# Mixture of experts on one core: the last two token groups with a Strassen second product, scaled left operands and kept weight parts

## The chip, the core and the metric

One Trainium2 chip, one of its cores. TensorE (PE in the profile) multiplies, with its own weight loads (PEld) beside it; VectorE (DVE), ScalarE (ACT) and GpSimd (POOL) work on tiles, and SyncE (SP) only issues transfers here. The metric is the device time of one execution in microseconds, the median of the runs.

## What is computed

Attention over 4 batches and 8 heads (queries pooled in pairs) gives 2304 tokens of 512 numbers, which pass through 8 experts. A gate P of 2304 x 8 is normalised by eight Sinkhorn rounds. Cut to what matters, with D = 512 and F = 1024:

```python
for e in range(8):
    h = np.maximum(x @ w1[e], 0.0)        # [2304, 1024]
    ye = h @ w2[e]                        # [2304, 512]
    out += P[:, e:e+1] * ye
```

All is float32. The kernel gets there on a faster matmul type (fp32r) by cutting each operand into a high part and a low remainder; a product is then three matmuls: high by high, high by low, low by high.

## The kernel before

`attention()` is a plan, a list of operations with costs that is put in order before the program is written. `moe()` is written in plain order, and a scheduler places its instructions. This case is about `moe()`.

The tokens go in G = 3 groups of TG = 768 (two halves of TH = 384). For each group the kernel walks over 32 steps, a step being one expert and one quarter of its hidden width (256 of 1024). The activations stay in one tile `x` [128, 4, 2304], with the model dimension on the partitions.

One step does this:

- **First product.** `product` makes x @ w1 for 256 hidden columns and 768 tokens by seven Strassen-Winograd block products of six matmuls each, 128x128 by 128x384 (L855 to L857, tile `psh`): 42 matmuls. The seven left operands are two parts of `w1s`, one more of it, and four sums (`w1t`, made by Pool in L133 to L136, for steps 2 to 8 of the first group by DVE). Each is cut into `w1h` (ACT, L147) and `w1l` (DVE, L152), in every group anew. The seven right operands are sums of x, cut into `xch` and `xcl` once per group (L100, L103; Pool makes the sums in L94).
- **Between.** ACT copies one block result (L870), DVE adds others (L875), and `hidden` cuts the rectified result into `hh` (ACT, L864) and `hl` (DVE, L865).
- **Second product.** Two steps make a window. In the window's wake `second` multiplies its hidden columns by w2, for each of the group's six tiles of 128 tokens 12 matmuls 128x128 by 128x512 (L885, tile `pso`): 72 in a window, 36 in a step. `w2s` is cut by ACT (L162) and DVE (L163). DVE takes each `pso` off, times its column of P, and adds it to `x` (L917; ACT in a group's first window, L911), which by then is free of the group's activations.
- **Loads and stores.** SP issues the loads of `w1s` (L119) and `w2s` (L125), 512 KB each, one of each per step, into one buffer each, and at a group's end the stores of the six token tiles (L919; the last tile in two halves, L904 and L905).

The reused buffers set the order: `w1s` can be loaded again once its cuts and sums are made, `w1h` and `w1l` have two buffers, `psh` and `pso` four each. The first product of a step needs only cuts made during the step before.

## Time and profile before

| | us |
|---|---|
| median of 3 runs | 1869.77 (1869.28 to 1870.08) |
| span of the profiled execution, first to last instruction | 1867.4 |
| PE busy | 1861.2 (100%) |
| DVE busy | 1438.6 (77%) |
| ACT busy | 825.5 (44%) |
| POOL busy | 509.2 (27%) |
| chain of work that ended last: PE | 98%, of it L885 42% |

The profiled execution's span is 2.4 us below the median. The attention part fills about the first 380 us, the three groups of 496 us each the rest. A profile's "busy" is a share over the whole span; what bounds a stage is seen from which wait ends last in it. A matmul's listed duration overlaps with its neighbours, so the cost of one is read from start to start.

### The profile page before, as it was taken

The numbers are of one execution on the slowest core, as the hardware profiler recorded it, in microseconds if no ns is written. First come the engines' busy times: TensorE is split into PE (matmuls) and PEld (weight loads), VectorE is DVE, ScalarE is ACT, GpSimd is POOL, SyncE is SP. The second block draws the span as 40 slices with busy tenths as digits, with TensorE's granted clock in tenths as the row PEclk, the third lists the DMA queues.
The fourth block names the chain that finished last, engine by engine and source line by source line (L and its number), as shares of the span: only waits on it lengthen the run. The fifth ranks groups of instructions, "written<-read, shape, count | busy, mean of one in ns | idle before, by whom it ended". The sixth has DMA issues, their size and how long they took to land.

```text
span 1867.4 us, 30970 instructions
## 1 busy us (share of the span) xinstructions
PE 1861.2 (100%) x11901; PEld 1673.9 (90%) x11901; DVE 1438.6 (77%) x2953; ACT 825.5 (44%) x1442; POOL 509.2 (27%) x504
## 2 busy tenths in 40 slices
PE   9999999999999999999999999999999999999999
PEld 8888888889999999999999999999899999999998
DVE  8999999799776767677777777777866777777774
ACT  7888887744333333333433333333433333333331
POOL 5555555410222222231222222223122222222210
PEclk9999999999999999999999999999999999999999
DMA  6777776322221212122212121212131212221211
GB/s 212 187 210 195 198 195 170 82 79 91 79 75 61 78 59 79 57 80 80 91 57 79 57 79 57 79 57 79 46 120 63 77 61 75 64 72 67 70 57 34
DMA packets 59524, 173.26 MB, mean 93 GB/s; under 512 B 11632, under 2 KB 21232, under 8 KB 59376
## 3 DMA queue, kind: packets, MB, share of 16 engines
q1 hardware_dynamic: 59088, 170.89, 30.7%
q8 instruction: 93, 1.52, 0.3%
q14 instruction: 55, 0.45, 0.1%
q10 hardware_dynamic: 288, 0.39, 0.1%
HBM read 134.81 MB, written 4.79 MB: 75 GB/s over the span
## 4 chain that ended last, share of the span: by engine, by line
PE 98%; DVE 1%; DMA 0%; ACT 0%; POOL 0%; issue 0%; POOLq 0%; ACTq 0%; SPq 0%
PE pso L885 42%; PE psh L857 12%; PE psh L855 12%; PE psh L856 12%; PE ps L530 7%; PE ps L607 4%; PE ps L639 3%; PE ps L653 3%; PE ps L658 1%; DVE w1l L152 0%; DMA w1s<-in_moe_w_dram 0%; DVE hl L865 0%; DMA qr<-in_q_dram 0%; PE ps L63 0%; ACT w1h L147 0%
## 5 line engine op out<-in xcount | busy, mean ns | idle before, releaser
L857 PE MATMUL psh<-xch,w1l 128*128 128x384 f32 x1344 | 450.2, 335 | 1.2 <-DVE w1l L152 1.2
L885 PE MATMUL pso<-w2h,hl 128*128 128x512 f32 x1156 | 450.7, 390 | 0.0
L885 PE MATMUL pso<-w2l,hh 128*128 128x512 f32 x1156 | 450.5, 390 | 0.0
L855 PE MATMUL psh<-xch,w1h 128*128 128x384 f32 x1344 | 450.1, 335 | 0.0
L856 PE MATMUL psh<-xcl,w1h 128*128 128x384 f32 x1344 | 449.6, 335 | 0.0
L885 PE MATMUL pso<-w2h,hh 128*128 128x512 f32 x1156 | 448.8, 388 | 0.0
L864 ACT ACTIVATE hh<-c 128x384 fp32r<-128x384 f32 x384 | 199.9, 522 | 377.5 <-DVE c L875 377.5
L133 POOL TENSOR_TENSOR w1t<-w1s 128x256 f32<-128x256 f32 x88 | 65.4, 743 | 1053.9 <-DMA w1s<-in_moe_w_dram 750.4
L917 DVE SCALAR_TENSOR_TENSOR x<-pso,PR,x 128x512 f32<-128x512 f32 x263 | 196.7, 748 | 158.2 <-PE pso L885 153.1
L885 PEld LDWEIGHTS pso<-w2h,hl 128*128 128x128 f32 x1156 | 217.0, 188 | 44.9
L855 PEld LDWEIGHTS psh<-xch,w1h 128*128 128x128 f32 x1344 | 252.3, 188 | 4.4 <-DVE c L875 0.4
L885 PEld LDWEIGHTS pso<-w2l,hh 128*128 128x128 f32 x1156 | 217.0, 188 | 43.1
L856 PEld LDWEIGHTS psh<-xcl,w1h 128*128 128x128 f32 x1344 | 252.3, 188 | 3.5
L885 PEld LDWEIGHTS pso<-w2h,hh 128*128 128x128 f32 x1156 | 217.1, 188 | 42.7
L857 PEld LDWEIGHTS psh<-xch,w1l 128*128 128x128 f32 x1344 | 252.2, 188 | 2.4 <-DVE w1l L152 2.4
L538 DVE TENSOR_SCALAR_CACHE_REDUCE E<-ps 128x384 f32<-128x384 f32 x432 | 214.9, 552 | 9.6 <-PE ps L530 8.6
L865 DVE SCALAR_TENSOR_TENSOR hl<-c,hh 128x384 fp32r<-128x384 f32 x384 | 211.3, 551 | 4.9 <-ACT hh L864 4.1
L870 ACT ACTIVATE p<-psh 128x384 f32<-128x384 f32 x96 | 47.2, 491 | 336.2 <-PE psh L857 335.0
L551 ACT ACTIVATE E<-E,st 128x1152 f32<-128x1152 f32 x144 | 179.9, 1262 | 16.0 <-DVE st L544 15.9
L163 DVE TENSOR_TENSOR w2l<-w2s,w2h 128x1024 fp32r<-128x1024 f32 x95 | 126.8, 1335 | 73.8 <-ACT w2h L162 73.8
L875 DVE TENSOR_TENSOR c<-psh,u 128x384 f32<-128x384 f32 x288 | 151.2, 554 | 42.1 <-PE psh L857 40.5
L162 ACT ACTIVATE w2h<-w2s 128x1024 fp32r<-128x1024 f32 x95 | 100.1, 1053 | 181.3 <-PE pso L885 181.3
(108 smaller groups left out, 2214.3 us busy)
## 6 DMA issues: line engine op xcount, KB each, us to landing
w1s<-in_moe_w_dram SPq DMA_DIRECT2D x96, 512.0 KB
w2s<-in_moe_w_dram SPq DMA_DIRECT2D x96, 512.0 KB
F<-T SPq DMA_DIRECT2D x168, 184.0 KB
qr<-in_q_dram SPq DMA_DIRECT2D x15, 640.0 KB
vt<-in_v_dram SPq DMA_DIRECT2D x16, 576.0 KB
kr<-in_k_dram SPq DMA_DIRECT2D x15, 576.0 KB
out_dram<-x SPq DMA_DIRECT2D x17, 256.0 KB
RB<-rd SPq DMA_DIRECT2D x32, 128.0 KB
```

The costliest lines, as they stand in the source:

```text
L163: self.tc.keep_in_program_order(self.nc.vector.tensor_tensor(out=lo, in0=self.raw2[k], in1=hi.bitcast(F32), op=ALU.subtract))
L530: nc.tensor.matmul(ps[h][:, :PK], D["qT", p][rows, x, t * P:(t + 1) * P], D["kT", p][rows, y, j * PK:(j + 1) * PK], start=(i == 0), stop=( ...
L538: nc.vector.tensor_scalar(out=D["E", m, h][:, j * PK:(j + 1) * PK], in0=D["sc", m, j][h][:, :PK], scalar1=0.0625, scalar2=None, op0=ALU.mu ...
L551: nc.scalar.activation(out=x, in_=x, func=ACTF.Exp, bias=D["st", m][:, h, 3:4], accum_out=sums[p % RS][:, col + h * QT:col + h * QT + 1])
L855: nc.tensor.matmul(ps, hi[:, a, c, :], blocks.xch[:, b, c, :], start=(c == 0), stop=False)
L856: nc.tensor.matmul(ps, hi[:, a, c, :], blocks.xcl[:, b, c, :], start=False, stop=False)
L857: nc.tensor.matmul(ps, lo[:, a, c, :], blocks.xch[:, b, c, :], start=False, stop=(c == 1))
L864: nc.scalar.activation(out=hh[:, fh, ts], in_=src, func=ACTF.Relu)
L865: nc.vector.scalar_tensor_tensor(out=hl[:, fh, ts], in0=src, scalar=0.0, in1=hh[:, fh, ts].bitcast(F32), op0=ALU.max, op1=ALU.subtract)
L875: nc.vector.tensor_tensor(out=y, in0=ps, in1=t, op=ALU.add)
L885: nc.tensor.matmul(ps, u[:, fh, ms], w[:, fh, ds], start=(n == 0), stop=(n == 11))
L917: nc.vector.scalar_tensor_tensor(out=a, in0=ps, scalar=PR[:, m, e:e + 1], in1=a, op0=ALU.mult, op1=ALU.add)
```

## The change

The first group stays as it was but for two things: w2 is laid out with its two halves of 256 columns apart, and after each step's cut both parts of w1 are written to a DRAM tile `w1c` (917.5 KB each, two transfers on SP ahead of the next load of `w1s`). P of groups 2 and 3 is turned once and written to DRAM (`spread`).

The last two groups leave `moe()` for a new function `late()`, a second plan:

- The high and low parts of w1 come back from DRAM in one load of 1.835 MB per step, into two buffers; nothing of w1 is summed or cut again.
- P of the expert is loaded as a row over all partitions (`pb`), and the rectified first product is multiplied by it (DVE, two operations of 384 and one of 2x384 columns per step). The sums between block products are carried by ACT copies from one PSUM bank to another; two more are added by DVE.
- The second product of a window is made by seven block products of twelve matmuls, 128x128 by 128x384 (L1193 in the new code): 84. Pool sums four blocks of w2 (512 wide) and four of h (768 wide); for each block product ACT cuts w_hi (512) and h_hi (768), DVE cuts w_lo (512) and h_lo (768), and DVE adds the result (768) to `x` (ACT in a group's first window).
- At a group's end seven sums of 768 columns (`join`, DVE or Pool) give the outputs, still with the model dimension on the partitions, and `finish` turns them by 24 matmuls against the identity, copies them out (12 copies of 256, ACT or DVE) and stores 12 pieces of 128 KB.

The diff's core:

```diff
@@ Weights.cut1, first group
             self.hi1(k)
             self.lo1(k)
+            t = self.kept[k] = self.cuts.tile([P, 2, 7, 2, P], F32, name=f"w1c{k}")
+            for i, y in enumerate(self.a[k]):
+                self.nc.sync.dma_start(out=t[:, i], in_=y.bitcast(F32))
...
+LATE_CAPS = dict(pb=2, w1=2, w2=2, w2t=1, hb=2, ht=1, hc=3, wc=3, e=2, mt=2, os=3)
...
+            def load_w1(k=k):
+                y = D0["w1", k] = tile("w1", [2, 7, 2, P], F32R)
+                nc.sync.dma_start(out=y.bitcast(F32), in_=wt.kept[k % (E * FQ)])
...
+                nc.vector.scalar_tensor_tensor(out=hb(b), in0=ps(n), scalar=0.0, in1=pb(0), op0=ALU.max, op1=ALU.mult)
...
+                nc.gpsimd.tensor_tensor(out=hblock(i), in0=D0[HB][:, a], in1=D0[HB][:, b], op=sub)
...
+                (nc.gpsimd if end else nc.vector).tensor_tensor(out=y[:, 1], in0=wsrc(), in1=y[:, 0].bitcast(F32), op=sub)
...
+                nc.vector.tensor_tensor(out=y[:, 1], in0=hblock(b), in1=y[:, 0].bitcast(F32), op=sub)
...
+                    for s in range(2):
+                        for y, z in ((0, 0), (0, 1), (1, 0)):
+                            nc.tensor.matmul(o, w[:, y, s, ds], v[:, z, s], start=(i == 0), stop=(i == 5))
```

How the instructions stand, at three places. First DVE in the steady part of a group. Before, about one step: sums (L875), the low part of h (`hl`, L865), the low parts of w1 and w2 (L152, L163), and `pso` taken off (L917).

```order
L875 TENSOR_TENSOR c_11466<-psh,c_11466 128x384
L865 SCALAR_TENSOR_TENSOR hl<-c_11475,hh 128x384
L152 TENSOR_TENSOR w1l<-w1s,w1h 128x512
L865 SCALAR_TENSOR_TENSOR hl<-c_11466,hh 128x384
L152 TENSOR_TENSOR w1l<-w1s,w1h 128x256
L152 TENSOR_TENSOR w1l<-w1t,w1h 128x1024
L917 SCALAR_TENSOR_TENSOR x<-pso,PR,x 128x4x128 x2
L163 TENSOR_TENSOR w2l<-w2s,w2h 128x1024
L917 SCALAR_TENSOR_TENSOR x<-pso,PR,x 128x4x128
L875 TENSOR_TENSOR c_11570<-psh,p_11561 128x384
```

In `late()`, under half of a window of 31 instructions: h scaled by P (L1089 and L1113, tile `hb`), w_lo and h_lo (L1170, L1180; tiles `wc`, `hc`, beside the sum tiles `w2t` and `ht`), a block product taken off (L1208, tile `mt`).

```order
L1170 TENSOR_TENSOR wc<-w2t,wc 128x512
L1113 SCALAR_TENSOR_TENSOR hb<-hb,pb 128x2x384
L1089 SCALAR_TENSOR_TENSOR hb<-bD,pb 128x384
L1208 TENSOR_TENSOR x<-mt,x 128x768
L1180 TENSOR_TENSOR hc<-hb,hc 128x768
L1170 TENSOR_TENSOR wc<-w2t,wc 128x512
L1180 TENSOR_TENSOR hc<-ht,hc 128x768
L1208 TENSOR_TENSOR x<-mt,x 128x768
L1170 TENSOR_TENSOR wc<-w2t,wc 128x512
L1180 TENSOR_TENSOR hc<-hb,hc 128x768
L1089 SCALAR_TENSOR_TENSOR hb<-bA,pb 128x384
```

The cuts of w1 are gone from DVE; wider cuts of h and of w2 stand there in turn with the results that are taken off.

Second, Pool beside it. Before, one step:

```order
L133 TENSOR_TENSOR w1t<-w1s 128x256 [waits DMAHW1_49,DVE_49]
L135 TENSOR_TENSOR w1t<-w1s 128x256
L134 TENSOR_TENSOR w1t<-w1t,w1s 128x256 [waits Pool_49]
L136 TENSOR_TENSOR w1t<-w1s,w1t 128x256 [waits Pool_49]
L133 TENSOR_TENSOR w1t<-w1s 128x256 [waits DMAHW3_49,DVE_49]
```

In `late()`, a window's eight:

```order
L1135 TENSOR_TENSOR w2t<-w_13610 128x512 [waits DMAHW4_49,DMAHW3_49,DVE_49]
L1135 TENSOR_TENSOR w2t<-w2t,w_13610 128x512 [waits Pool_49]
L1135 TENSOR_TENSOR w2t<-w_13610 128x512
L1135 TENSOR_TENSOR w2t<-w_13610,w2t 128x512 [waits Pool_49]
L1151 TENSOR_TENSOR hb<-hb 128x768 [waits DVE_49]
L1151 TENSOR_TENSOR ht<-hb 128x768 [waits DVE_49]
L1151 TENSOR_TENSOR hb<-hb 128x768 [waits Pool_49]
L1151 TENSOR_TENSOR hb<-hb 128x768 [waits DVE_49,Pool_49]
```

Eight short sums for two steps have become four of double and four of triple width, the last four fed by DVE.

Third, SP where the first group ends. Before, the stores of the finished tiles (L919) lie among the loads:

```order
L125 DMA w2s<-in_moe_w_dram 128x1024
L119 DMA w1s<-in_moe_w_dram 128x1024
L125 DMA w2s<-in_moe_w_dram 128x1024
L919 DMA out_dram<-x 512x1x128 x3
L119 DMA w1s<-in_moe_w_dram 128x1024
L919 DMA out_dram<-x 512x1x128
L125 DMA w2s<-in_moe_w_dram 128x1024
L919 DMA out_dram<-x 512x1x128 x2
```

Now, from the first group's last steps on (kept parts L163, loads L122 and L128, stores L913, then `pb` L1037, the kept parts back L1051, w2 L1043):

```order
L122 DMA w1s<-in_moe_w_dram 128x1024
L128 DMA w2s<-in_moe_w_dram 128x1024
L163 DMA w1c_10346<-w1h 128x1792
L163 DMA w1c_10346<-w1l 128x1792
L128 DMA w2s<-in_moe_w_dram 128x1024
L913 DMA out_dram<-x 512x1x128 x5
L1037 DMA pb<-spread 128x768
L913 DMA out_dram<-x 512x1x128
L1051 DMA w_10650<-w1c_5992 128x3584
L1043 DMA w_10658<-in_moe_w_dram 128x1024 x2
L1051 DMA w_10673<-w1c_6084 128x3584
```

In the first group two writes now stand ahead of each load of `w1s`; at its end all six stores, each behind DVE, stand ahead of the first load of `late()`.

## Rows read from the trace of the kernel before

**Rows 1.** the page: busy us (share), and the chain that ended last

```profile
PE 1861.2 (100%) x11901; PEld 1673.9 (90%) x11901; DVE 1438.6 (77%) x2953; ACT 825.5 (44%) x1442; POOL 509.2 (27%) x504
...
PE 98%; DVE 1%; DMA 0%; ACT 0%; POOL 0%; issue 0%; POOLq 0%; ACTq 0%; SPq 0%
```

**Rows 2.** chain of waits, 1000 to 1035: start us, us, engine, tile, line

```profile
1002.19 8.20 PE pso L885 x36
1017.69 8.20 PE pso L885 x36
```

**Rows 3.** engines in windows, steady: us, busy us (count), PEclk, DMA share, GB/s

```profile
1000.00:1015.50 15.50, 15.50 (x80) 14.06 (x79) 11.27 (x18) 5.33 (x9) 3.72 (x4) 1.00 0.21 69
```

**Rows 4.** DVE by line and form: count | busy us, mean ns | idle

```profile
L152 DVE TENSOR_TENSOR w1l<-w1s,w1h 128x512 fp32r<-128x512 f32 x95 | 66.3, 698 | 0.1
L103 DVE TENSOR_TENSOR xcl<-x,xch 128x768 fp32r<-128x768 f32 x9 | 8.4, 950 | 0.0
L875 DVE TENSOR_TENSOR c<-psh,p 128x384 f32<-128x384 f32 x96 | 53.5, 557 | 80.6 <-PE psh L857 80.0 <-ACT w1h L147 0.5
L913 DVE TENSOR_TENSOR x<-pso,x 128x512 f32<-128x512 f32 x6 | 3.9, 687 | 0.0
L865 DVE SCALAR_TENSOR_TENSOR hl<-c,hh 128x384 fp32r<-128x384 f32 x384 | 211.3, 551 | 4.9 <-ACT hh L864 4.1
L163 DVE TENSOR_TENSOR w2l<-w2s,w2h 128x1024 fp32r<-128x1024 f32 x95 | 126.8, 1335 | 73.8 <-ACT w2h L162 73.8
```

**Rows 5.** POOL in order of time, 1287 to 1294: start us, us, engine, line

```profile
1288.95 0.74 POOL L134 TENSOR_TENSOR w1t<-w1t,w1s 128x256 f32<-128x256 f32 x1
1289.77 1.61 POOL L136 TENSOR_TENSOR w1t<-w1s,w1t 128x256 f32<-128x256 f32 x1
1291.33 1.85 POOL L94 TENSOR_TENSOR xt<-x,xt 128x768 f32<-128x768 f32 x1
```

**Rows 6.** DVE in order of time, 1289 to 1302

```profile
1289.28 1.49 DVE L163 TENSOR_TENSOR w2l<-w2s,w2h 128x1024 fp32r<-128x1024 f32 x1 [1.71 <-ACT w2h L162]
1290.69 0.74 DVE L917 SCALAR_TENSOR_TENSOR x<-pso,PR,x 128x512 f32<-128x512 f32 x1
1291.72 0.56 DVE L875 TENSOR_TENSOR c<-psh,p 128x384 f32<-128x384 f32 x1 [0.29 <-PE psh L857]
1300.33 0.75 DVE L917 SCALAR_TENSOR_TENSOR x<-pso,PR,x 128x512 f32<-128x512 f32 x1
1300.99 1.22 DVE L163 TENSOR_TENSOR w2l<-w2s,w2h 128x1024 fp32r<-128x1024 f32 x1
```

**Rows 7.** POOL, then DVE, 362 to 372

```profile
366.24 1.83 POOL L94 TENSOR_TENSOR xt<-x 128x768 f32<-128x768 f32 x1
368.02 2.13 POOL L707 TENSOR_TENSOR x<-x,RB 128x576 f32<-128x576 f32 x1
...
367.09 3.89 DVE L103 TENSOR_TENSOR xcl<-xt,xch 128x768 fp32r<-128x768 f32 x2
```

**Rows 8.** ACT by line and form: count | busy us, mean ns | idle

```profile
L100 ACT ACTIVATE xch<-xt 128x768 fp32r<-128x768 f32 x8 | 6.7, 840 | 0.6 <-POOL xt L94 0.3
```

**Rows 9.** SP, then POOL, in order of time, 1000 to 1017

```profile
1004.80 0.33 SPq L119 DMA_DIRECT2D w1s<-in_moe_w_dram  x1
...
1008.40 0.73 POOL L133 TENSOR_TENSOR w1t<-w1s 128x256 f32<-128x256 f32 x1 [12.62 <-DMA w1s<-in_moe_w_dram]
```

**Rows 10.** engines in windows: with stores and loads; after the end

```profile
878.00:880.00 2.00, 2.00 (x12) 1.84 (x11) 0.75 (x1) 0.00 (x0) 1.92 (x3) 1.00 0.91 301
1866.00:1867.40 1.40, 0.00 (x0) 0.00 (x0) 0.00 (x0) 0.00 (x0) 0.00 (x0) 0.53 0.06 18
```

**Rows 11.** PE at the start, in order of time; chain, 240 to 256

```profile
1.56 3.79 PE L401 MATMUL ps<-ident 128*128 128x128 f32 x16 [1.56 <-POOL ident masks.py:199]
...
243.89 2.81 PE ps L607 x24
```

**Rows 12.** the last piece of the chain of waits

```profile
1864.19 0.48 DVE x L904
```

More of the change, by code (lines that the diff above doesn't have):

```diff
@@ L43, in attention_moe @@
         tc.tile_pool(name="const", bufs=1) as const,
[L44 removed]
+        tc.tile_pool(name="cuts", bufs=1, space=bass.MemoryType.DRAM) as cuts,
     ):
+        stage = tc.alloc_tile_pool(name="stage", bufs=1, reuse_waits="tile")
         edge.tile([P, 8], F32, name="edge")
@@ L50, in attention_moe @@
         PR = const.tile([P, NT, E], F32, name="PR")
-        wt = Weights(tc, stage, w1, w2)
+        wt = Weights(tc, stage, w1, w2, cuts)
         blocks = Blocks(tc, stage, x)
@@ L56, in attention_moe @@
         moe(tc, out, x, ident, wg, PR, blocks, wt)
+        stage.release()
+        late(tc, out, x, ident, blocks, wt)
         blocks.pool.release()
@@ L106, with __init__ @@
 class Weights:
-    def __init__(self, tc, stage, w1, w2):
-        self.tc, self.nc, self.stage, self.w1, self.w2 = tc, tc.nc, stage, w1, w2
-        self.raw1, self.raw2, self.a, self.b, self.sums = {}, {}, {}, {}, {}
-        self.steps = G * E * FQ
+    def __init__(self, tc, stage, w1, w2, cuts):
+        self.tc, self.nc, self.stage, self.w1, self.w2, self.cuts = tc, tc.nc, stage, w1, w2, cuts
+        self.raw1, self.raw2, self.a, self.b, self.sums, self.kept = {}, {}, {}, {}, {}, {}
+        self.steps = E * FQ
     def load1(self, k, tag="w1s"):
@@ L876, in plus, with terms @@
             return y
-        def terms(ps, ks, ms, ds):
+        def terms(ps, ks, ms):
             n = 0
@@ L882, in terms @@
                     hh, hl = hids[k]
-                    hi, lo = wt.b[k]
+                    hi, lo = (y.rearrange("p a (b d) -> p a b d", b=2)[:, :, fh] for y in wt.b[k])
                     for u, w in ((hh, hi), (hh, lo), (hl, hi)):
-                        nc.tensor.matmul(ps, u[:, fh, ms], w[:, fh, ds], start=(n == 0), stop=(n == 11))
+                        nc.tensor.matmul(ps, u[:, fh, ms], w, start=(n == 0), stop=(n == 11))
                         n += 1
@@ L894, in second @@
                     pass
-            m = g * MT + i
-            ms = slice(i * P, (i + 1) * P)
-            a = x[:, :, m * P:(m + 1) * P]
-            last = (half + 1) % (FQ * E // 2) == 0
-            if m == NT - 1 and last:
-                for c in range(0, ND, 2):
-                    ps = ps2.tile([P, ND, P], F32, name="pso", tag="ps2")
-                    terms(ps[:, :2], ks, ms, slice(c * P, (c + 2) * P))
-                    y = a[:, c:c + 2]
-                    nc.vector.scalar_tensor_tensor(out=y, in0=ps[:, :2], scalar=PR[:, m, e:e + 1], in1=y, op0=ALU.mult, op1=ALU.add)
-                    nc.sync.dma_start(out=out[m * P:(m + 1) * P, c * P:(c + 2) * P].rearrange("p (c d) -> p c d", c=2), in_=y)
-                return
@@ L907, in second @@
-            ps = ps2.tile([P, ND, P], F32, name="pso", tag="ps2")
-            terms(ps, ks, ms, slice(0, D))
-            first = half % (FQ * E // 2) == 0
-            if first:
-                nc.scalar.activation(out=a, in_=ps, func=ACTF.Copy, scale=1.0 if g == 0 else PR[:, m, e:e + 1])
-            elif g == 0 and e == 0:
+            a = x[:, :, i * P:(i + 1) * P]
+            ps = ps2.tile([P, ND, P], F32, name="pso", tag="ps2")
+            terms(ps, ks, slice(i * P, (i + 1) * P))
+            if half == 0:
+                nc.scalar.activation(out=a, in_=ps, func=ACTF.Copy)
+            elif e == 0:
@@ L913, in second @@
                 nc.vector.tensor_tensor(out=a, in0=ps, in1=a, op=ALU.add)
             else:
-                if g == 0 and half == FQ // 2:
-                    nc.vector.tensor_scalar(out=a, in0=a, scalar1=PR[:, m, 0:1], scalar2=None, op0=ALU.mult)
-                nc.vector.scalar_tensor_tensor(out=a, in0=ps, scalar=PR[:, m, e:e + 1], in1=a, op0=ALU.mult, op1=ALU.add)
-            if last:
-                nc.sync.dma_start(out=out[m * P:(m + 1) * P, :].rearrange("p (c d) -> p c d", c=ND), in_=a)
+                if half == FQ // 2:
+                    nc.vector.tensor_scalar(out=a, in0=a, scalar1=PR[:, i, 0:1], scalar2=None, op0=ALU.mult)
@@ new lines, in second, with spread @@
+                nc.vector.scalar_tensor_tensor(out=a, in0=ps, scalar=PR[:, i, e:e + 1], in1=a, op0=ALU.mult, op1=ALU.add)
+            if half == E * FQ // 2 - 1:
+                nc.sync.dma_start(out=out[i * P:(i + 1) * P, :].rearrange("p (c d) -> p c d", c=ND), in_=a)
+        def spread():
+            n = (NT - MT) * E
+            ps = ps2.tile([P, D], F32, name="psp", tag="ps2")
+            nc.tensor.transpose(ps[:n, :P], PR[:, MT:].rearrange("p n e -> p (n e)"), ident)
+            t = tmp.tile([P, TH], F32, name="c21", tag="c21")[:n, :P]
+            nc.scalar.activation(out=t, in_=ps[:n, :P], func=ACTF.Copy)
+            y = wt.spread = wt.cuts.tile([E, NT - MT, P], F32, name="spread")
+            nc.sync.dma_start(out=y.rearrange("e n t -> n e t"), in_=t)
@@ L928, in moe @@
         for k in range(wt.steps):
-            g, r = divmod(k, FQ * E)
-            if g and r == 0:
-                for i in (0, 1, 4, 5, 3, 6, 2):
-                    blocks.hi(g, i)
-                    blocks.lo(g, i)
-                some_second(3)
             hids[k] = [hid.tile([P, 2, TG], F32R, name=nm, tag=nm) for nm in ("hh", "hl")]
@@ L956, in moe @@
             wt.load2(k + 1)
-            if g + 1 < G and r >= FQ * E - 4:
-                blocks.add(g + 1, (3, 4, 6, 5)[r - FQ * E + 4], nc.gpsimd)
+            if k >= wt.steps - 4:
+                blocks.add(1, (3, 4, 6, 5)[k - wt.steps + 4], nc.gpsimd)
             if k == 0:
```

297 lines of the change are left out of this document (288 added, 9 removed).

## The prediction

> **What bounds the kernel now.** I read the page first, then the chain of waits, then the engines in windows, then durations by line, then engines in order of time.
>
> The page says that PE is busy 1861.2 of 1867.4 us and that 98% of the chain of waits is PE [rows 1]. So only fewer PE microseconds help, or stalls hurt. In the steady part the chain shows what a step is made of: the 36 matmuls of 512 columns take 8.20 us, the next such piece starts 15.50 us later [rows 2]. The second product thus costs 8.20 / 36 = 0.228 us a matmul, and the 42 matmuls of 384 columns between the pieces 7.30 / 42 = 0.174 us each. A window of two steps is 31.0 us. Beside PE the other engines have room: in 15.5 us DVE works 11.27, ACT 5.33, POOL 3.72 [rows 3].
>
> The page's median lies 2.4 us above the span; I sum against the span and add that.
>
> **What PE saves.** A window of `late()` has 84 first-product matmuls and 84 second-product matmuls, all of 384 columns: 168 x 0.174 = 29.2 us against 31.0. Over 32 windows that is 32 x 1.8 = **-57.6**. The first group keeps its count.
>
> **What paces the late windows.** This term decides the case. A window has 31 DVE instructions. By the rows of like shape: seven w_lo of 512 (0.68 to 0.70), seven h_lo of 768 (0.95), two scalings of 768 (0.95 taken), eight of 384 out of PSUM (0.56), seven block products taken off. The last form is not in the trace: 384 columns out of PSUM take 0.557, 512 take 0.687, so 768 about 0.95, an estimate [rows 4]. DVE instructions in a row follow each other 0.08 to 0.09 us sooner than their durations say: the one at 1300.33 lasts 0.75, the next starts 0.66 later [rows 6]. So: 7 x 0.60 + 7 x 0.87 + 2 x 0.87 + 8 x 0.475 + 7 x 0.87 = 21.9 us. That alone would hide under 29.2.
>
> But Pool works more: four sums of 768 at 1.85 and four of 512, between 0.74 for 256 and 1.85 for 768, so about 1.29: 12.6 us a window [rows 5]. And the two engines shut each other out. A 1024-wide `w2l`, which reads two SBUF operands, takes 1.22 alone (1300.99), but 1.49 at 1289.28, where Pool's L134 still ran until 1289.69; it ends 1.08 after that. Pool's L136, due at 1289.77, then takes 1.61 instead of 0.74 and ends 0.61 after DVE's. At 367.09 two `xcl` take 3.89 instead of 1.9, one behind each of Pool's two, whose second grows too [rows 5 to 7]. DVE instructions that read PSUM and one SBUF operand run beside Pool undisturbed: 0.74 at 1290.69, 0.56 at 1291.72 under Pool's 1.85 [rows 5, 6]. So an instruction with two SBUF operands and one of Pool run one after the other, each for its whole length, and the one that asked first goes first.
>
> Sixteen of the 31 (w_lo, h_lo, the two scalings) are of that kind. The Trainium skill, page "SBUF — State Buffer", section "Who interferes with whom", says the same as a rule: a VectorE instruction with two SBUF inputs and a GpSimd one that reads SBUF hold the shared ports exclusively, whoever issues first. If that rule did not hold, this term would be zero and the sum 1849.
>
> I laid a window out by hand in the written order, with these durations, a blocked DVE instruction ending its length less 0.13 after Pool's and a blocked Pool one its length less 0.15 after DVE's, PE at 0.174. Seven DVE instructions find Pool in the way and wait 0.5, 1.6, 1.6, 0.8, 0.6, 1.0 and 1.0: 7.2 us. Two more wait about 0.5 each for ACT's cut of h (0.84 [rows 8]). 21.9 + 7.2 + 1.0 = 30.1 us a round. The place where PE notices: the product into bank D waits until the scaling has emptied that bank; DVE comes to it 0.8 us late, then the round repeats with the same lag. So a window is 30.1, not 29.2. It is not at work in the two first windows of a group, where ACT takes results off, nor in the last, which stands in the tail below: 29 x 0.9 = **+26**. Bounds: 0, if Pool's sums fall into DVE's pauses; +52, if a window is no shorter than today's 31.0.
>
> **The start of the late part.** Today the next group's cuts are made beforehand and PE runs on. Now SP's order puts the first load of kept parts behind the sixth store, so behind the last result that DVE takes off. From the last matmul to DVE's end 1.2 us (0.43 and 0.75), issue of the store 0.5, then the load. 512 KB took 3.6 us from issue to Pool's start [rows 9]; 1.31 MB more at 0.30 to 0.33 MB/us (the stretch with stores and a load moved 301 GB/s [rows 10]) makes it 7.6 to 8. Sum 9.6. Queued behind that load is everything of `late()`; PE has nothing else. PE then starts at half clock: after the last matmul the granted clock falls, mean 0.53 of full over the last 1.4 us, and at the kernel's start 16 matmuls took 3.79 us where 24 of the same shape later took 2.81 [rows 10, 11]: 3.79 - 16 x 0.117 = 1.9 lost. The second and third loads come just in time, 0.7. Two seed matmuls 0.35. **+12.5**, bounds 9 and 17.
>
> **Between the last two groups.** The join (seven sums of 768), the cuts of x (seven of 768 with two SBUF operands), Pool's four sums of x and the copies come on top for DVE, seven results less since ACT takes them: 6.1 + 5 + 3 - 6.1 + 4 for blocking = 12, of which the neighbouring windows' slack takes some; the group's 24 transposes run in PE's pauses. **+8**, bounds 3 and 16.
>
> **The end.** In the last window Pool makes w_lo too: 7 x 1.25 + 4 x 1.8 = 16, and DVE's seven h_lo 6, one after the other, 22 us against PE's 14.6. Then the last block is taken off, the join, transposes, copies into three buffers, twelve stores of 0.4 us issue. Laid out the same way the last store lands about 33 us after the last first-product matmul. Today's way to end (PE to the last matmul, then 0.48 and the store, 3.4 us [rows 12]) would give 19.1 there. **+14**, bounds 9 and 19.
>
> **The first group.** A step must now write 1.835 MB and load 0.5 before Pool can sum. From ACT's last cut: issue and start 1.2, 2.36 MB at 301 GB/s 7.9, landing 0.9, Pool 2.9 to 4 (it meets more DVE work there), ACT's cut 1.05: 14 to 15 of the 15.5 that a step has. **+2**, bounds 0 and 35 (at 250 GB/s up to 1.1 us a step are missing).
>
> **The sum.** -57.6 + 26 + 12.5 + 8 + 14 + 2 = +5. Span 1872, time **1875**. This kernel's runs tell about 0.2%, some 3.7 us, from no change.
>
> **Rivals.**
>
> 1. *PE stays the bound in the late windows* and the change is faster. For it: DVE's 15 PSUM instructions (9.7 us a window) and its pauses are places where Pool works for free, 24.5 us of exclusive work fit into 29.2, and only 0.8 us must be found. Against: Pool's last three sums come one behind the other just when DVE has five cuts in a row. It decides when DVE waits less than 6.3 of the 7.2 us. Then the 26 fall away: 1849.
> 2. *The first group's loop of write, load, sum and cut* outruns the step: below some 280 GB/s each of 30 steps pays, at 250 GB/s up to 33 us in all: 1890 to 1908. Against: the stretch with 301 GB/s moved short pieces, the new ones are 7 KB a partition. SP's order has both writes ahead of the load.
> 3. *DVE's waits are longer*, 31.0 or more a window, nothing saved in the steady part: 1900. For it: ACT's cuts queue behind Pool's as well.
> 4. *The change doesn't do what it says*: each window waits for its loads, because the order on SP holds them behind buffers that come free late. 2.9 MB in 29 us is 100 GB/s beside the 301 seen; against it. 1900 and more.
>
> A page's rule on the pause at the start: the Trainium skill, "TensorE: Matmul & The Clock Gate", section "What's actually happening", has an idle array fall to half its clock. The two rows above agree in size; without it the sum would be 2 us less.
>
> **How the numbers follow.** Forecast (windows of about 30.1): 0.50, 1860 to 1888 by its terms' bounds, mostly above 1873.5. Rival 1: 0.30. Rival 2: 0.11. Rival 3: 0.06. Rival 4: 0.03. Faster by over 0.2% (below 1866): rival 1 and a little of the forecast, 0.34. Within: 0.16 from the forecast's middle. Slower: the rest, 0.50. Leaving out the far ends of rivals 1 to 4, the range is 1845 to 1900.
>
> **What would show it.** In the new profile: steady windows of 30 us instead of 29.2, with PE idle before the products and DVE named as releaser; DVE's two-operand cuts longer than 0.70 and 0.95 in the mean, Pool's 768-wide sums longer than 1.85; a pause of PE of about 10 us between the groups with a half clock behind it; the end some 14 us after the last second-product matmul. I am wrong if cuts beside Pool keep their length, if PE is busy throughout, or if the first group's steps exceed 15.5 us.

## The result, and the profile after

The changed kernel takes **1884.03 us** (median of 4 runs, 1883.58 to 1885.85) against 1869.61 (4 runs, 1869.28 to 1870.08) beside it: a ratio of 1.0078, interval 1.0063 to 1.0092. It is slower, by 14.4 us. Its profiled execution has a span of 1881.8 us, 14.4 more than before. The forecast was 1875, 5 us slower, with a chance of 0.50 on slower and 0.34 on faster: range and direction hold, the direction at even odds, and the size is 9 us short.

The page of the changed kernel: busy us (share of the span) and count for each engine, then the chain of work that ended last.

```profile
PE 1825.7 (97%) x12324; PEld 1714.4 (91%) x12324; DVE 1676.1 (89%) x2800; ACT 915.9 (49%) x1587; POOL 804.7 (43%) x519
...
DVE 19%; POOL 2%; issue 2%; ACT 2%; PE 1%; POOLq 0%; DMA 0%; SPq 0%; ACTq 0%; DVEq 0%
```

Against [rows 1]: PE is busy 35.5 us less, DVE 238 us more, POOL 296 us more, and in the chain, once 98% PE, DVE stands ahead of all others. The shares of this chain add up to only 26%: it reaches back no further than 1401.6 us, so it speaks for the last group alone. (In the run with the start mended, below, the chain is followed over the whole span: 48% PE, 41% DVE.) PE's own list of waits says where it stood still: engine, tile and line that waited, who released it, us in all, times, longest.

```profile
PE bD L1022 <- DVE hb L1089: 24.0, 30, 2.1
PE bA L1022 <- DMA w<-w1c: 9.9, 1, 9.9
PE mt L1193 <- DVE hc L1180: 6.6, 6, 1.7
```

The first row is mostly the steady part (27 of the 30 waits): PE waits before the product into bank D, on the DVE instruction that empties that bank (L1089). The second row is the start of the late part, one wait of 9.9. In order of time (start, us, engine, line, tile; in brackets the idle time before) the steady wait comes back every 30.2 us, with the same length:

```profile
1005.17 0.44 PE L1022 MATMUL bD<-xch,w 128*128 128x384 f32 x1 [0.79 <-DVE hb L1089]
...
1035.38 0.44 PE L1022 MATMUL bD<-xch,w 128*128 128x384 f32 x1 [0.79 <-DVE hb L1089]
```

From one scaling L1113 to the second next, 26 of the 31 window lengths are 30.2 us and the last is 29.6 (27 with a lag in them); the three around the change from the third group to the last are 32.0, 36.0 and 36.1, the first is 27.6. The engines in windows, same columns as [rows 3]: a stretch of twelve steady windows, the three long ones, and the end.

```profile
974.90:1337.30 362.40, 352.93 (x2016) 349.10 (x2016) 351.50 (x374) 157.84 (x266) 176.33 (x97) 1.00 0.45 164
1337.30:1441.40 104.10, 94.59 (x528) 90.64 (x528) 97.03 (x102) 50.67 (x87) 59.96 (x30) 0.98 0.44 157
...
1846.20:1881.80 35.60, 23.05 (x113) 20.12 (x111) 23.07 (x26) 10.37 (x18) 25.31 (x12) 0.86 0.14 45
```

In the steady part DVE is busy 351.5 of 362.4 us and PE has gaps: the two have changed places. Why DVE is so full is in its groups by line and form (count, busy us, mean ns, idle before), with two of Pool's below:

```profile
L1180 DVE TENSOR_TENSOR hc<-hb,hc 128x768 fp32r<-128x768 f32 x192 | 232.4, 1211 | 29.3 <-ACT hc L1175 29.2
L1208 DVE TENSOR_TENSOR x<-mt,x 128x768 f32<-128x768 f32 x209 | 197.6, 945 | 2.1 <-PE mt L1193 2.1
L1170 DVE TENSOR_TENSOR wc<-w2t,wc 128x512 fp32r<-128x512 f32 x124 | 138.4, 1117 | 2.3 <-ACT wc L1163 2.3
L1170 DVE TENSOR_TENSOR wc<-w,wc 128x512 fp32r<-128x512 f32 x93 | 125.8, 1352 | 0.6 <-ACT wc L1163 0.6
L1180 DVE TENSOR_TENSOR hc<-ht,hc 128x768 fp32r<-128x768 f32 x32 | 78.8, 2464 | 0.1
L1113 DVE SCALAR_TENSOR_TENSOR hb<-hb,pb 128x768 f32<-128x768 f32 x64 | 75.8, 1184 | 1.1
L1089 DVE SCALAR_TENSOR_TENSOR hb<-bD,pb 128x384 f32<-128x384 f32 x64 | 34.9, 545 | 0.1
```

```profile
L1151 POOL TENSOR_TENSOR hb<-hb 128x768 f32<-128x768 f32 x96 | 208.2, 2169 | 50.4 <-DVE hc L1180 45.6
L1135 POOL TENSOR_TENSOR w2t<-w 128x512 f32<-128x512 f32 x64 | 105.6, 1650 | 192.7 <-DVE wc L1170 165.1 <-DMA w<-in_moe_w_dram 27.6
```

Forms that read two SBUF tiles are long: the 512-wide cuts 1117 and 1352 where the same shape took 698 before, the 768-wide ones 1211 and 2464 where it took 950 [rows 4]. Forms with one operand in PSUM are not: 945 for 768 columns (L1208), 545 for 384 (L1089).

### The profile page after: what moved, and what is told of

Read it like the earlier page. It is cut to its first block, busy times and chain, and to the rows that moved or that the text cites. A ratio compares the mean times of both kernels' runs of the same rounds, so it can differ in the third digit from the quotient of the medians.

```text
span 1881.8 us, 31877 instructions
## 1 busy us (share of the span) xinstructions
PE 1825.7 (97%) x12324; PEld 1714.4 (91%) x12324; DVE 1676.1 (89%) x2800; ACT 915.9 (49%) x1587; POOL 804.7 (43%) x519
## 5 line engine op out<-in xcount | busy, mean ns | idle before, releaser
L1193 PE MATMUL mt<-hc,wc 128*128 128x384 f32 x2688 | 538.8, 335 | 9.4 <-DVE hc L1180 6.6
L1193 PEld LDWEIGHTS mt<-hc,wc 128*128 128x128 f32 x2688 | 473.5, 188 | 12.6 <-DVE hc L1180 8.6
L1180 DVE TENSOR_TENSOR hc<-hb,hc 128x768 fp32r<-128x768 f32 x192 | 232.4, 1211 | 29.3 <-ACT hc L1175 29.2
L1151 POOL TENSOR_TENSOR hb<-hb 128x768 f32<-128x768 f32 x96 | 208.2, 2169 | 50.4 <-DVE hc L1180 45.6
L1208 DVE TENSOR_TENSOR x<-mt,x 128x768 f32<-128x768 f32 x211 | 198.6, 942 | 2.2 <-PE mt L1193 2.1
L863 PE MATMUL psh<-xch,w1l 128*128 128x384 f32 x448 | 150.1, 336 | 0.8 <-DVE w1l L155 0.8
L861 PE MATMUL psh<-xch,w1h 128*128 128x384 f32 x448 | 150.2, 335 | 0.0
L891 PE MATMUL pso<-w2h,hl 128*128 128x512 f32 x384 | 150.0, 391 | 0.0
L891 PE MATMUL pso<-w2l,hh 128*128 128x512 f32 x384 | 149.9, 390 | 0.0
L862 PE MATMUL psh<-xcl,w1h 128*128 128x384 f32 x448 | 149.9, 335 | 0.0
L891 PE MATMUL pso<-w2h,hh 128*128 128x512 f32 x384 | 149.5, 389 | 0.0
L136 POOL TENSOR_TENSOR w1t<-w1s 128x256 f32<-128x256 f32 x24 | 17.7, 738 | 296.1 <-DMA w1s<-in_moe_w_dram 286.3
L1170 DVE TENSOR_TENSOR wc<-w2t,wc 128x512 fp32r<-128x512 f32 x124 | 138.4, 1117 | 2.3 <-ACT wc L1163 2.3
```

Of the source, the lines that this page charges most:

```text
L861: nc.tensor.matmul(ps, hi[:, a, c, :], blocks.xch[:, b, c, :], start=(c == 0), stop=False)
L863: nc.tensor.matmul(ps, lo[:, a, c, :], blocks.xch[:, b, c, :], start=False, stop=(c == 1))
L891: nc.tensor.matmul(ps, u[:, fh, ms], w, start=(n == 0), stop=(n == 11))
L1151: nc.gpsimd.tensor_tensor(out=hblock(i), in0=D0[HB][:, a], in1=D0[HB][:, b], op=sub)
L1170: (nc.gpsimd if end else nc.vector).tensor_tensor(out=y[:, 1], in0=wsrc(), in1=y[:, 0].bitcast(F32), op=sub)
L1180: nc.vector.tensor_tensor(out=y[:, 1], in0=hblock(b), in1=y[:, 0].bitcast(F32), op=sub)
```

## The experiments

The theory: DVE's instructions with two SBUF operands and Pool's sums shut each other out, so that DVE paces the windows, and the rest is a pause at the start, a crowded change of groups and a longer end. The main rival: what DVE has to do is simply too much, or loads and writes are late. Of every run but the last two there is one execution, beside one of the kernel before; "the changed kernel" below stands for 1884.03 us, span 1881.8. What an edit does not touch differs by a microsecond or two between executions: the pause at the start is 8.4 to 10.3 us in the six runs that leave the start as it is, and the end, from the last L1113 on, is 36.35 to 37.6 in the four that leave the end as it is. Differences of that size are not read as effects.

**Without Pool's four sums of w2.** The blocks are read raw in their place.

```diff
-                nc.gpsimd.tensor_tensor(out=get(i), in0=get(a), in1=get(b), op=how)
+                pass
...
-            wsrc = lambda: D0[W2T][:, a - 3] if a > 2 else raw(a)
+            wsrc = lambda: raw(a - 3 if a > 2 else a)
```

> The changed kernel without Pool's four sums of w2 (512 wide) in each late window; the blocks that need a sum read a plain quarter of w2 instead, so that part of the computation is left out. All else as in the changed kernel (window 30.20 us, PE waits 0.79 us in each for the scaling into bank D, 1884.0 us). If DVE loses its time behind Pool (the forecast's mechanism), three of its seven waits go, 2.4 us where about 1.0 is missing: windows of 29.2 to 29.4, no wait at bank D, 24 us less in 25 windows, about 1860. If DVE's own length and its waits for ACT's cuts set the pace, nothing moves: 30.2, 1884. If the transfers slow PE, nothing moves either.

1849.66 us, span 1847.9: 34 less, where about 24 were expected. Nothing was taken from DVE; its 31 instructions a window are the same, yet the windows are 29.12 us and PE no longer waits for bank D in them. The stretch of the steady part, columns as before:

```profile
974.90:1313.00 338.10, 338.10 (x1953) 338.10 (x1952) 306.52 (x359) 157.60 (x257) 99.87 (x48) 1.00 0.48 174
```

PE is busy without a gap, and DVE is at 91% where it was at 97%. So it is Pool's sums of w2 that made DVE late; whether by their reading or otherwise, the next run tells. The ten microseconds more than expected come from two places: a steady window gave back 1.08, not 0.8 to 0.9, 29 us in all, and the three long windows gave another 5.2 (30.0, 33.6, 35.3).

The 1.08 also corrects how a wait is read. The row of the wait says 0.79. But matmuls overlap: they start every 0.173 us and last 0.33. The wait is counted from the modelled end of the last one, and the first one after it is 0.28 ahead of the next instead of 0.17 (1005.17 and 1005.45 in the trace). PE loses some 0.3 more than the row shows.

**Pool writes but does not read.** Each of the eight sums becomes two writes of a constant into the same tile (743 ns each for 768 columns, 528 for 512), so Pool's place in the order stays, and it works four fifths as long as its sums of 1.85 and 1.29 would alone, without reading.

```diff
-                nc.gpsimd.tensor_tensor(out=get(i), in0=get(a), in1=get(b), op=how)
+                for _ in range(2):
+                    nc.gpsimd.memset(get(i), 0.01)
...
-                nc.gpsimd.tensor_tensor(out=hblock(i), in0=D0[HB][:, a], in1=D0[HB][:, b], op=sub)
+                for _ in range(2):
+                    nc.gpsimd.memset(hblock(i), 0.01)
```

> The changed kernel with each of Pool's eight sums in a late window made into two writes of a constant to the same place, which read nothing; the sums are left out. Pool stays busy at the same places in the order, about as long (two fills of 768 are estimated at 1.2 to 1.5 us against 1.85). If DVE and Pool exclude each other only where both read SBUF, DVE's cuts fall to their lengths alone (0.70 for w_lo, 0.95 for h_lo) and a window is 29.2, about 1860. If it is Pool's being busy, or who waits for Pool's results, that holds DVE, the cuts stay near 1.1 to 1.3 us in the mean and a window above 29.6.

1840.9 us, span 1839.1. DVE by line and form, in this run (the edit moves the line numbers by two), and one of Pool's groups:

```profile
L1182 DVE TENSOR_TENSOR hc<-hb,hc 128x768 fp32r<-128x768 f32 x192 | 185.5, 967 | 24.9 <-ACT hc L1177 24.6
L1172 DVE TENSOR_TENSOR wc<-w2t,wc 128x512 fp32r<-128x512 f32 x124 | 85.9, 693 | 5.7 <-ACT wc L1165 5.7
L1172 DVE TENSOR_TENSOR wc<-w,wc 128x512 fp32r<-128x512 f32 x93 | 63.4, 682 | 3.2 <-ACT wc L1165 3.2
L1182 DVE TENSOR_TENSOR hc<-ht,hc 128x768 fp32r<-128x768 f32 x32 | 31.0, 969 | 0.7 <-ACT hc L1177 0.6
```

```profile
L1153 POOL MEMSET hb<- 128x768 f32 x192 | 142.6, 743 | 394.2 <-DVE hb L1113 300.9 <-DVE hc L1182 87.7
```

All forms are back at the durations of the kernel before: 693 and 682 for 1117 and 1352, 967 and 969 for 1211 and 2464. DVE's order and Pool's are unchanged; what is gone is the reading of these eight sums. This is what the Trainium skill, "SBUF — State Buffer", section "Who interferes with whom", says: a DVE instruction with two SBUF inputs contends with a GpSimd instruction that reads SBUF, and not with one that only writes it. The trace agrees on both halves, 2464 ns beside a reader and 969 beside a writer.

The time is 19 us below the 1860 that was expected: a window gives back 1.08 here too, and the run takes exclusion away in two other places as well. The three long windows shrink to 29.95, 30.9 and 32.5: of the 16.7 us that they cost over three of 29.12, at least 10.7 were this exclusion. And the end, from the last L1113 on, takes 33.6 us instead of 36.35, 2.7 less. Both are lower bounds: Pool's sums of `join` (L1240, five at the change of groups and three at the end) and its seven w_lo of the last window still read here, and cuts of DVE still take 2.13 beside them (1359.32 and 1361.85).

**The first loads of the kept parts on ACT's queue**, past the stores.

```diff
-            @op("SP", 7000, T + 14 * s - 18, w=[("w1", k)], new=[(("w1", k), "w1")], lat=2500)
+            @op("ACT" if k < 2 else "SP", 500 if k < 2 else 7000, T + 14 * s - (48 if k < 2 else 18), w=[("w1", k)], new=[(("w1", k), "w1")], lat=2500)
...
-                nc.sync.dma_start(out=y.bitcast(F32), in_=wt.kept[k % (E * FQ)])
+                (nc.scalar if k < 2 else nc.sync).dma_start(out=y.bitcast(F32), in_=wt.kept[k % (E * FQ)])
```

> The changed kernel with the first two loads of kept w1 parts issued from ACT's queue, where nothing stands ahead of them, instead of behind the six stores on SP. If the order on SP is the cause of the pause (9.88 us of PE idle before the first late product, then 12 matmuls at half clock, 1.8 us), PE waits under 1.5 us there, the half clock goes too, and the time falls by 10 to 12 us, to about 1873. If the load would be late anyway (its buffer comes free late, or P's rows and w2 are the last to land), it falls by less than 5.

1879.74 us: 4.3 less, not the ten expected. The pause of 9.9 is gone from PE's waits, but others have come. PE, then ACT, in order of time:

```profile
872.02 0.34 PE L1022 MATMUL bA<-xch,w 128*128 128x384 f32 x1
...
879.72 0.44 PE L1022 MATMUL bA<-xch,w 128*128 128x384 f32 x1 [1.26 <-DVE hb L1089]
...
883.45 0.69 PE L1022 MATMUL bD<-xch,w 128*128 128x384 f32 x1 [2.40 <-ACT bD L1076]
```

```profile
882.38 0.63 ACT L1163 ACTIVATE wc<-w 128x512 fp32r<-128x512 f32 x1 [6.54 <-DMA w<-in_moe_w_dram]
882.92 0.47 ACT L1076 ACTIVATE bD<-bC 128x384 f32<-128x384 f32 x1
```

PE starts at 872.02 instead of 881.62. But the row of P (L1037) and w2 (L1043) still stand behind the stores on SP, and ACT's order has a cut of w2 ahead of a copy between banks (L1076) that PE needs. ACT waits 6.54 us for that load, and everything behind it waits too. The first L1113 comes at 884.78 instead of 890.9, 6.1 sooner: about half of the pause and its half clock had moved to another engine. Part of the 6.1 does not show in the time because the end, which the edit leaves alone, took 37.6 us.

**The parts of w1 written in two steps only**, later loads read those two again.

```diff
-            t = self.kept[k] = self.cuts.tile([P, 2, 7, 2, P], F32, name=f"w1c{k}")
-            for i, y in enumerate(self.a[k]):
+            t = self.kept[k] = self.cuts.tile([P, 2, 7, 2, P], F32, name=f"w1c{k}") if k < 2 else self.kept[k % 2]
+            for i, y in enumerate(self.a[k] if k < 2 else ()):
```

> The changed kernel with the parts of w1 written to DRAM in the first two steps only; the late windows read these two again and again, so most of the kept parts are left out. The late loads are as many and as large. The first group took as long with the writes as without by the trace (0 us instead of the 2 of the forecast), so: no change, 1883 to 1885. If the writes cost the first group or the late part anything, the time falls by that much.

1883.51 us, span 1881.7: no change. A stretch of the first group, of the changed kernel and then of this one:

```profile
700.00:860.00 160.00, 160.00 (x804) 144.69 (x803) 122.89 (x183) 53.78 (x90) 42.32 (x40) 1.00 0.41 148
```

```profile
700.00:860.00 160.00, 160.00 (x803) 144.67 (x802) 116.23 (x183) 53.44 (x90) 40.48 (x37) 1.00 0.16 53
```

The writes are 95 GB/s of traffic and cost PE nothing; the first group ends at 870.92 us without them and at 871.23 with them. The rival on the first group's loop falls.

**No cuts of x for the last group**: the third group's are used again.

```diff
-                cut_x(g)
+                pass
```

> The changed kernel without the sums and cuts of x for the last group, which works on the cuts of the group before; that part of the computation is left out. Between the two late groups the changed kernel spends 16 us over PE's own pace (104.0 us from the wait at 1337.4 to that at 1441.4 for 504 matmuls and 24 transposes), where the forecast had 8. If the cuts of x (seven of DVE, four sums of Pool) are half of it or more, the stretch falls by 7 to 10 us. If the join and the transposes are the larger part, it falls by less than 4.

1879.71 us: 4.3 less. The three long windows become 30.2, 32.7 and 37.7, together 3.5 less, which is the second expectation (less than 4): the cuts and sums of x are a fifth of the 16.7. The larger part is what remains, the join, the transposes and the copies beside the usual load. The parts overlap: the exclusion of the run above sits in all of them.

**The sums of w2 made once, in the first group**, in place in the raw tile, written to DRAM and read back in every late window.

```diff
+        y = self.raw2[k].rearrange("p h d -> p (h d)")
+        r = [y[:, o:o + 256] for o in (0, 256, 768, 512)]
+        e = self.nc.gpsimd
+        e.tensor_tensor(out=r[2], in0=r[3], in1=r[2], op=ALU.add)
+        e.tensor_tensor(out=r[3], in0=r[0], in1=r[3], op=ALU.subtract)
+        e.tensor_tensor(out=r[0], in0=r[2], in1=r[0], op=ALU.subtract)
+        e.tensor_tensor(out=r[1], in0=r[1], in1=r[0], op=ALU.subtract)
+        self.nc.sync.dma_start(out=self.kept2[k // 2][:, k % 2], in_=y)
...
-            wsum(i, a, b, how, T - 9 + n)
+                nc.sync.dma_start(out=y, in_=wt.kept2[j % PW])
```

> The changed kernel with the four sums of w2 made once, by Pool in the first group in place of the loaded block, written to DRAM (512 KB a step) and read back in the late windows (1 MB each); nothing is left out. Leaving those sums out took 34 us off (1849.7). If Pool's work beside DVE is what costs and not the data, this keeps that gain and does the full work: 1848 to 1853. If the first group's steps get longer by the extra write and Pool's 2.9 us a step, or a load comes late, part of it goes: 1855 to 1875.

1965.23 us, a clear miss. The late part did as it should: windows of 29.12, and from its first L1113 to its last 920.7 us instead of 954.6, 33.9 less. But its first L1113 comes at 1006.0 instead of 890.9: the first group takes 115 us more. Waits of PE and of SP:

```profile
PE pso L902 <- ACT w2h L169: 41.7, 4, 34.3
```

```profile
SPq L181 <- POOL w2s L180: 147.9, 30, 19.0
SPq L129 <- DMA w2c<-w2s: 57.8, 29, 3.1
```

The raw tile is now cut, summed by Pool and written out before the next load may overwrite it, and SP, which issues all of this in one order, stands 147.9 us behind Pool's last sum (L180) with the loads of w1 queued behind. The first thirteen steps lose some 76 us between them (34.3 in one wait for w2's cut, in the eighth), and from the seventeenth on a step of 15.5 us takes 18.1, which makes up the rest: the write L181 is issued at 652.59 and, twelve steps on, at 869.68.

**The same with the start on ACT's queue and six store buffers** (`os=6`).

```diff
-LATE_CAPS = dict(pb=2, w1=2, w2=2, w2t=1, hb=2, ht=1, hc=3, wc=3, e=2, mt=2, os=3)
+LATE_CAPS = dict(pb=2, w1=2, w2=2, w2t=1, hb=2, ht=1, hc=3, wc=3, e=2, mt=2, os=6)
```

> The kernel with the w2 sums made in the first group, and besides the first two loads of kept w1 on ACT's queue and six buffers instead of three for the turned output tiles. The loads on ACT's queue took 4 us off the changed kernel, since ACT's copies then stood behind a cut of w2 that waited for its load (6.5 us); the three last output tiles waited some 1.5 us for their buffers. So 5 to 6 us under the kernel with the w2 sums alone. If that one gains nothing, only the 5 to 6 remain.

1965.36 us, no gain. The first pause shrinks from 10.2 to 2.2 us, but the first window grows from 29.2 to 32.6 and PE waits 1.9 us for ACT's copy into bank D (L1087), the copy it waited for in the run with this start alone. The first load is not the only thing that PE is waiting for.

**The last window's low parts of w2 on DVE** instead of Pool.

```diff
-            @op("Pool" if end else "DVE", pool(512) if end else dve(512), slot - 6,
+            @op("DVE", dve(512), slot - 6,
...
-                (nc.gpsimd if end else nc.vector).tensor_tensor(out=y[:, 1], in0=wsrc(), in1=y[:, 0].bitcast(F32), op=sub)
+                nc.vector.tensor_tensor(out=y[:, 1], in0=wsrc(), in1=y[:, 0].bitcast(F32), op=sub)
```

> The changed kernel with the seven w_lo of the last window back on DVE instead of Pool. In the changed kernel the end takes 35.6 us from the last first-product matmul, 17 us more than PE's work and the old end. If the end is paced by what DVE and Pool cannot do at once (Pool 16 us, DVE's two-operand cuts 6), moving 9 us of Pool's to 4 us of DVE's shortens it by 3 to 5 us. If the last block's chain (result, join, transposes, copies, stores) alone makes the end, it changes by less than 1.

1888.79 us, 4.8 more where less was expected. From the last L1113 to the end it takes 39.25 us, not 36.35. The chain that ended last, in order of time:

```profile
1858.54 1.62 DVE hc L1180
1860.16 0.60 DVE wc L1170
1860.76 0.87 DVE x L1208
```

Here the chain stays on DVE from 1849.2 to 1870.7: cut, cut, result, one behind the other, also where no sum of Pool is in the way and the cuts are short (0.60; 0.87 for the result). In the changed kernel the chain of the same stretch runs through Pool instead: its sums of h and its w_lo, and at the very end three sums of `join`, 2.5 us each.

```profile
1852.80 2.51 POOL hb L1151
...
1865.12 2.51 POOL x L1238
```

Giving DVE the cuts was the wrong way: by the two chains the engine that has them sets the pace, and DVE has seven h_lo and seven results beside them where Pool has four sums. (Of the 5.2 us that the span is longer, 1.5 lie ahead of the first L1113, where the edit touches nothing and executions differ by as much: in the runs with this start the first L1113 comes at 889.4 to 892.4.)

**The start mended**: P's first row and the first two loads of kept parts on ACT's queue, the planner told that the first w2 of the late part comes late (so that ACT's cut of it stands further back), six store buffers. Beside the edits on the loads and on `os` shown above:

```diff
-                nc.sync.dma_start(out=y, in_=wt.spread[e, n:n + MT].rearrange("n t -> (n t)").unsqueeze(0).to_broadcast([P, TG]))
+                (nc.scalar if j == 0 else nc.sync).dma_start(out=y, in_=wt.spread[e, n:n + MT].rearrange("n t -> (n t)").unsqueeze(0).to_broadcast([P, TG]))
...
-        @op("SP", 4000, T - 16, w=[("w2", j)], new=[(("w2", j), "w2")], lat=2500)
+        @op("SP", 4000, T - 16, w=[("w2", j)], new=[(("w2", j), "w2")], lat=9000 if j == 0 else 2500)
```

> The changed kernel with its start mended further: the first row of P and the first two loads of kept w1 are issued from ACT's queue ahead of ACT's late work, the plan is told that the first w2 lands late, so that ACT's copies between banks come before the cuts of w2, and the output has six buffers. Nothing is left out. The start costs the changed kernel about 13 us (9.9 idle, the half clock, small waits); with the loads on ACT alone 5 came back and ACT behind a cut of w2 (6.5 us) held the rest. If that reading is right, 10 to 12 us come back, and 1 more at the end: 1871 to 1874. If P's row or w1 still lands late, 1877 to 1880, as with the loads alone.

1873.65 us (median of 10 runs) against 1870.1 (13 runs), ratio 1.002, interval 1.001 to 1.003: 10.4 less than the changed kernel, as expected. The first L1113 comes at 878.56 instead of 890.9, 12.3 sooner; the first window takes 1.9 of it back. With the pause taken out the kernel is still 0.2% slower than before: what eats the 60 us that the matmuls gain is the pace of the windows (29), the change of groups (17) and the end (17), more than the start.

The chain of this run, which reaches back over the whole span:

```profile
PE 48%; DVE 41%; POOL 4%; issue 4%; ACT 3%; DMA 0%; POOLq 0%; ACTq 0%; DVEq 0%
```

**The start mended, and the third group's sums of w2 kept** in DRAM for the last group: there Pool has only the sums of h to make.

```diff
+            @op("SP", 800, T + 11, r=[("wl", j, 4)], use=[W2T], lat=2500)
+            def keep_w2t():
+                y = wt.kept2[j] = wt.cuts.tile([P, 4, 2, 256], F32, name=f"w2c{j}")
+                nc.sync.dma_start(out=y, in_=D0[W2T])
...
+                y = D0[W2T] = tile("w2t", [4, 2, 256])
+                nc.sync.dma_start(out=y, in_=wt.kept2[j - PW])
```

> The same, and the four sums of w2 that Pool makes in each window of the second group are written to DRAM (1 MB a window) and read back in the last group, where Pool then makes only the sums of h; nothing is left out. If Pool's work beside DVE sets the pace, the second group stays at 30.2 us a window and the last group goes to 29.2 to 29.3: 13 to 16 us less than the kernel without this, about 1857. If the kept sums cost as much as they save (a load behind a waiting write on SP), no less than 1868.

**1856.16 us** (median of 4 runs) against 1870.1 (13 runs), ratio 0.9926, interval 0.9911 to 0.9940. This beats both kernels. It is 17.5 less than the run without this edit, a little over the 13 to 16 expected. The steady stretch of the third group and that of the last, in one profile:

```profile
920.00:1340.00 420.00, 411.54 (x2352) 406.93 (x2351) 408.15 (x432) 187.98 (x315) 212.57 (x112) 1.00 0.57 200
1445.00:1775.00 330.00, 330.00 (x1906) 330.00 (x1905) 300.94 (x353) 152.92 (x250) 94.22 (x45) 1.00 0.54 202
```

```profile
PE bD L1023 <- DVE hb L1090: 9.8, 13, 1.8
```

It is the test of the theory within one run. The same program runs in both groups but for Pool's four sums: in the third, windows of 30.09 with a wait for bank D of about 0.7 in each, in the last 29.12 with PE busy 330.0 of 330.0 us, and the waits down from 27 (the run without this edit) to thirteen. The price, 1 MB written per window and read back, is hidden: neither kind of window is longer than it would be without it.

## Why the prediction was right, point by point

By the prediction's own terms, with PE's pure window of 29.12 from the run without w2 sums (168 matmuls of 0.173), counted from the end of the first group's work (871.6 before: its last second-product matmuls end at 878.9, with 7.3 of the next group's first product ahead of them; 871.2 now):

| Term | Predicted | Measured | From |
|---|---|---|---|
| matmuls | -57.6 | -60.2 | 32 x (31.0 - 29.12) |
| DVE's pace in the windows | +26 | +29.2 | 27 x 1.08 |
| the start | +12.5 | +12.0 | 881.62 - 871.23, and 1.6 of half clock |
| between the last groups | +8 | +16.7 | 104.06 - 3 x 29.12 |
| the end | +14 | +17.2 | 35.6 - 14.6 of PE, less 3.8 that the end took before |
| the first group | +2 | -0.4 | 871.2 - 871.6 |
| sum | +5 | +14.5 | span: +14.4 |

- **What bounds the kernel.** Right. PE paced it before; after, DVE does in the late windows: 41% of the whole chain in the run with the start mended, where PE's 48% are about the length of what comes before `late()`.
- **The matmuls.** Right to 2.6 us: 0.1733 a matmul, not 0.174.
- **The pace.** Right in mechanism, place and size. 30.1 us a window were laid out, 30.20 came; a lag of 0.8 us before the product into bank D was foreseen, 0.79 is in the row. It was not luck: the seven waits that were laid out (0.5, 1.6, 1.6, 0.8, 0.6, 1.0, 1.0) are in DVE's round, in that order. From 1019.30 on the seven instructions last 0.55, 1.65, 1.65, 0.84, 0.52, 1.00 and 1.00 us longer than their own 0.68 or 0.95, 7.2 in all; the two waits for ACT's cut, 0.5 each in the forecast, are 0.37 and 0.51. The first three of the seven, and Pool beside them:

```profile
1019.30 1.50 DVE L1180 TENSOR_TENSOR hc<-hb,hc 128x768 fp32r<-128x768 f32 x1
1020.72 2.33 DVE L1170 TENSOR_TENSOR wc<-w2t,wc 128x512 fp32r<-128x512 f32 x1
1022.97 2.60 DVE L1180 TENSOR_TENSOR hc<-ht,hc 128x768 fp32r<-128x768 f32 x1
```

```profile
1018.13 1.85 POOL L1151 TENSOR_TENSOR ht<-hb 128x768 f32<-128x768 f32 x1 [8.62 <-DVE hb L1113]
1020.06 4.70 POOL L1151 TENSOR_TENSOR hb<-hb 128x768 f32<-128x768 f32 x2
```

  The rule behind it (an instruction with two SBUF operands and one of Pool run in turn) could be read before from a handful of chance meetings [rows 5 to 7], and Pool that writes without reading confirms it. In number the term is 3 too small: a window lost 1.08, not 0.9, since the round is 0.1 longer than laid out and PE's own window 0.08 shorter than 29.2 (in 27 windows, where 29 were counted). The second of these is the 2.6 that the matmuls gained beyond the forecast, so the two errors nearly cancel. The estimate of 0.95 for the product taken off was 0.945.
- **The start.** Right. The pause was put at 9.6 and is 9.88, and the half clock behind it is there. PE, in order of time:

```profile
871.40 0.34 PE L1027 MATMUL bC<-xch 128*128 128x384 f32 x1
881.62 0.69 PE L1022 MATMUL bA<-xch,w 128*128 128x384 f32 x1 [9.88 <-DMA w<-w1c]
...
883.06 0.52 PE L1022 MATMUL bA<-xcl,w 128*128 128x384 f32 x1
883.38 0.52 PE L1022 MATMUL bA<-xch,w 128*128 128x384 f32 x1
...
886.18 0.33 PE L1022 MATMUL bB<-xcl,w 128*128 128x384 f32 x1
886.35 0.33 PE L1022 MATMUL bB<-xch,w 128*128 128x384 f32 x1
```

  Starts are 0.32 apart up to 885.3, which is the lower level of the clock (1.2 GHz; the mean granted from 874 to 886 is 0.57), then 0.17: twelve matmuls take 3.68 us for 2.08, 1.6 lost, where 1.9 was taken from the kernel's first instants [rows 11]. The Trainium skill, "TensorE: Matmul & The Clock Gate", section "What's actually happening", has an idle array fall to half its clock; these rows agree. SP's order was the cause that the prediction named, in the rows of SP:

```profile
859.67 10.35 SPq L913 DMA_DIRECT2D out_dram<-x  x5
870.13 0.56 SPq L1037 DMA_DIRECT2D pb<-spread  x1
872.21 0.55 SPq L913 DMA_DIRECT2D out_dram<-x  x1
872.84 0.58 SPq L1051 DMA_DIRECT2D w<-w1c  x1
```

- **Between the last groups.** The place is right, the size is half. This is the term that was mis-sized most, and the steps in it that failed are two. "12, of which the neighbouring windows' slack takes some" gave 8: DVE, which the prediction had full in one paragraph, was to absorb work in the next. It is busy 97.0 of the 104.1 us, and its 7 idle ones lie behind the crowd, at 1402 to 1412, where it waits for ACT. And "the group's 24 transposes run in PE's pauses" put them at nothing: but for one wait of 0.8 ahead of the first, they stand between matmuls that follow without a pause (two at 1403.84, two at 1405.11), and they take 2.7 us, start to start. The other 14 of the 16.7 are what PE loses where it waits for DVE's h_lo, scalings, results and join, and at least 10.7 of the 16.7 go when Pool's eight sums a window no longer read.
- **The end.** 3 short. PE's last second-product matmul ends at 1868.15, 13.65 before the end, as foreseen ("some 14 us"). It is the last window ahead of it that is longer, 22 us from the last first-product matmul instead of the 19 that are left of the 33 laid out. The prediction's own count for it, Pool's 16 and DVE's 6 in turn, was 22. (It took 19.1 for today's way to end, where its parts, 14.6 and 3.4, give 18.0; with that the term would have been 15.) In the trace Pool works there almost without a pause from 1846.5 to 1864.2, four sums of h and five w_lo in 17.7 us, and the last h_lo and PE's last matmuls follow. How much of that is exclusion stays open: with Pool's sums of h and w2 not reading the end is 2.7 shorter, but its w_lo and its join still read in that run; with the cuts on DVE it is longer, and the chain DVE's.
- **The first group.** Its +2 was not needed: loads, sums and cuts came in time with 148 GB/s, and leaving the writes out changes nothing.
- **The rivals.** That PE stays the bound (1849) fell: DVE finds Pool in the way too often, and PE shows it. Had it come, the measured terms without the pace would give 1855, where 1849 stood. Its measure for the fall holds: it needed DVE waits under 6.3 of 7.2 us a window, and 7.2 came. (The 9.7 us that it gives DVE's 15 PSUM instructions are 9.9 by the lengths listed; nothing hangs on it.) Longer DVE waits (31.0 and more) did not come, and loads do not pace the windows.

What stays open: how the end divides between exclusion and the work of one engine, and how the waits at the change of groups divide between join, cuts of x and copies. Of the 6 us that the three long windows still cost when Pool's eight sums do not read, 2.2 are the transposes; most of the rest is PE's waits for DVE (1.2 before bank D and 0.8 before a transpose by the rows), beside a join that still reads.
